# A two-layer-pair kernel on one core: the third chunk's second layers by Strassen's scheme, and its 1/rms applied behind the first layer

## The chip, the core and the metric

The kernel runs on one core of a Trainium2 chip. TensorE (PE) multiplies, VectorE (DVE), ScalarE (ACT) and GpSimd (POOL) work elementwise, SyncE (SP) issues the DMAs. The metric is the device time of one execution in microseconds; less is better.

## The reference

Attention with forget gates feeds two gated feed-forward networks; the second normalises its input by its root mean square.

```python
def _moe_ref(x, w_a, w_b, w_out):
    a = x @ w_a
    b = x @ w_b
    return (a * b @ w_out).astype(np.float32)
...
def _moe2_ref(x, w_gate, w_val, w_out, rms_g):
    rms = np.sqrt(np.mean(x * x, axis=-1, keepdims=True) + 1e-06)
    xn = x / rms * rms_g
    g = xn @ w_gate
    silu = g * (1.0 / (1.0 + np.exp(-g)))
    val = xn @ w_val
    return (silu * val @ w_out).astype(np.float32)
```

There are 2304 tokens, a model width of 512 and an inner width of 1536. Weights arrive as float64 and outputs are float32.

## The kernel before, in words

Tokens stand in columns. They are cut in three chunks of 576, 704 and 1024 (`CHUNKS`), and each chunk goes through both networks. `PHASES` gives the order of these passes: (network 0, chunk 0), (0, 1), (1, 0), (1, 1), (0, 2), (1, 2), numbered 0 to 5. The last two, phases 4 and 5, are the third chunk's.

Every float32 operand is split into a high part, rounded by ScalarE, and a low part, the remainder, on VectorE or GpSimd. A product is three matmuls (`triple`, L790 to L792): high by high, high by low, low by high.

The first layer of a chunk other than chunk 0 (`plan_wino`) uses Strassen's scheme in Winograd's form: for each f of 12 (128 inner rows each) seven blocks P1 to P7 of six matmuls stand for the two products with the two first weights, over two halves of columns (512 each in phases 4 and 5). `expand` makes the combinations of X that they read (sums L900, splits L907 and L910) in cells of E. PSUM bank m1 takes P1, P6, P5, P3 of one f in turn and is read between them; m2 takes P7 and P4, m3 P2. ScalarE takes a first value (L1027), VectorE adds the next (L1036), in phase 5 ScalarE's tanh (L1045) and L1049 make the gate, L1075 or L1036 the product, and L1126 and L1129 split it into G.

The second layer (`y_block`) is plain. It runs after each third of the f (`THIRDS`, four f each, `QF`): for four blocks i of 128 outputs and two column halves s, 12 matmuls (4 rows of G by three) into one bank; `out_part` puts the result into X (ACT for the first third, L824 or L826 for the others). In phase 3 the last third of the second layer is not done in place but held (`HELD`) and run at the end of phase 4, around the norm of phase 5. Its weights and those of the third chunk's y blocks come in two `wy` tiles.

The norm (`normed`) sums squares over partitions by matmuls (L1166), takes 1/sqrt by Newton steps on VectorE (L1162, L1178, L1181), spreads the result with diagonals (L1195) and multiplies X by it and by the gain (L1206). For phase 5 it stands between the second layer of phase 4 and the expansion of X.

Each engine runs its instructions in one fixed order. `Plan.order` lays it out ahead of the run: every operation has a cost, reads, writes and a due time (`prio`), and the earliest startable one goes next. An operation marked EITHER goes to VectorE or GpSimd.

Of the kernel before, what the change touches and what calls it, by code (L numbers as in the profile page):

```python
# [40 lines left out]

GRAIN = 32
# [6 lines left out]
    (((3, ALL, 0),), ((2, 0.1, 1.0, 0.7), (3, 0.1, 0.95, 0.3)), 20000),  # L49
# [16 lines left out]
HELD = 3  # L66
# [6 lines left out]
P_BUFS, PT_BUFS, RAW_BUFS, WY_BUFS = 4, 4, 2, 2  # L73
# [66 lines left out]
class Buf:  # L140
# [6 lines left out]
    def make(self):  # L147
        pool, shape, dtype = self.spec
        pool = pool() if callable(pool) else pool
        self.tile = pool.tile(shape, dtype, tag=self.tag, bufs=self.bufs, name=self.name)  # L150

# [166 lines left out]
class Kernel:  # L318
# [117 lines left out]

    def swap_3(self):
# [3 lines left out]
        self.G.append(pool.tile([128, 8 * WIDE], F32R, name="G2"))  # L441
# [35 lines left out]
    def cell_keys(self, b, t, c, m):  # L477
        return self.keys("E", *self.cell_at(b, t, c, m), slice(0, WIDTH[c]))

    @staticmethod  # L480
    def g_at(t, f, c):
        return int(c == 2), (t * QF + f % QF) * (WIDE if c == 2 else NARROW)

    def g(self, t, f, c, cols):
        x, o = self.g_at(t, f, c)
        return self.G[x][:, o + cols.start : o + cols.stop]

    def g_keys(self, t, f, c, cols):
        return self.keys("G", *self.g_at(t, f, c), cols)

# [5 lines left out]
    def blocks(self, p):  # L496
# [13 lines left out]
        out = [("P1", 0), ("P7", 0), ("P2", 0)]  # L510
        for f in range(FT):
            out += [("P6", f), ("P4", f)]
            nxt = [[(x, f + 1)] if f + 1 < FT else [] for x in ("P1", "P7", "P2")]
# [13 lines left out]
    def block_cost(self, p, x):  # L527
        c = PHASES[HELD if x[0] == "held" else p][1]
        if x[0] in ("y", "ab", "held"):
            return 12 * mm(size(c, x[-1]))  # L530
# [263 lines left out]
    def y_block(self, p, c, i, q, s, w, acc, t, e, first, last, m, after=()):  # L794
# [3 lines left out]
        for a, b in ((0, QF - 1), (QF - 1, QF)):  # L798

            def block(*_, a=a, b=b):  # L800
# [5 lines left out]
            made = self.op(  # L806
                PE, 3 * (b - a) * mm(n), block, reads=["late", (w, 0), (w, 1), *reads], writes=[acc],
                prio=t + 3000 + 0.75 * (e - t) * (a > 0), after=after,
            )
        self.out_part(p, m, c, i, s, first, last, acc, e)  # L810
        return made

    def out_part(self, p, m, c, i, s, first, last, acc, e):
# [6 lines left out]
        scale = 0.5 if m else 1.0  # L820

# [22 lines left out]
        ssq, keys_ = self.total(c, cols), self.total_keys(c, s)  # L844
        if i == 0:
# [3 lines left out]
            )  # L849
            return  # L850
# [5 lines left out]
        op(  # L856
            DVE, dve(n), lambda: nc.vector.tensor_tensor(out=ssq(), in0=ssq(), in1=q.tile[:, :n], op=ALU.add),
            reads=[q], writes=keys_, prio=e + 800, port=True,
        )
# [11 lines left out]
    def expand(self, p):  # L871
# [15 lines left out]
        x = lambda k, n: self.xc[c][:, 2 * k : 2 * k + 2, n * h : n * h + h]  # L887
        if m:
            has = lambda k, n: [y for i in (2 * k, 2 * k + 1) for y in pieces(c, n, "x1", c, i)]
        else:  # L890
            has = lambda k, n: [y for y, i, cols in self.x_parts[0, c] if i // 2 == k and cols.start < n * h + h and cols.stop > n * h]
        late = self.late2(p)
        of = lambda b, t: self.cell(b, t, c, m)
        used = self.used_x[m, c] = []
        cost = (dve(2 * h), pool2(2 * h))

        def add(d, out, a, b, how, reads, writes, start=True):
# [6 lines left out]
        def parts(b, src, reads, d):  # L904
# [7 lines left out]
            hi, lo = (self.cell_keys(b, t, c, m) for t in range(2))  # L912
            used.append(op(ACT, act(2 * h), high, reads=[*reads, *late], writes=hi, prio=t0 + d))
# [3 lines left out]
        h11, h12, h21, h22 = (has(k, n) for k in range(2) for n in range(2))  # L917
        at = lambda *k: ("at", c, m, *k)

        for k, n, y in ((0, 0, h11), (0, 1, h12), (1, 0, h21), (1, 1, h22)):  # L920
            self.plan.writer[at(k, n)] = op(None, 0, lambda: None, reads=y)
# [12 lines left out]


    def plan_wino(self, p, m, c):
# [4 lines left out]
        loaded, banks, a, turn, y_seen = {}, {}, {}, 0, []  # L941
        last_p = max(k for k, x in enumerate(blocks) if x[0] not in ("y", "held"))
# [25 lines left out]
        for k, x in enumerate(blocks):  # L968
# [4 lines left out]
            if x[0] in ("y", "held"):  # L973
                _, i, q, s = x
                m_, c_ = PHASES[HELD] if x[0] == "held" else (m, c)
                if s == 0:
                    all_ = x[0] == "y" and q == THIRDS - 1 and self.adjoins(p + 1)
                    w = loaded["y", m_, i, q] = self.w_tile() if p < SWAP_AT or all_ else self.tile(
                        [128, 2, 2, 256], "wy", WY_BUFS, F32R, pool=lambda: self.late_3
                    )  # L980
                    j = 2 * FT + 3 * i + q
                    op(
                        SP, 480, lambda z, m_=m_, j=j: nc.sync.dma_start(self.flat(z), self.wd[m_][j]),
                        reads=[("wd", m_, j), *([] if p < SWAP_AT else ["late3"])], writes=[(w, 0), (w, 1)], prio=t - 9000, nbytes=524288,
                    )
                w = loaded["y", m_, i, q]
                tags = ("m2", "m3") if q < THIRDS - 1 else ("m2", "m3", "m1", "m1")
                if p >= SWAP_AT:
                    acc = self.bank(*(("s", S_BANKS), ("tp", TP_BANKS))[turn % 2])
                else:  # L990
                    acc = self.m_bank(tags[turn % len(tags)])
                turn += 1
                after = [y_seen[KT - 1]] if x[0] == "held" else ()
                made = self.y_block(p, c_, i, q, s, w, acc, t, e, q == 0, q == THIRDS - 1, m_, after)
                if q == THIRDS - 1:
                    y_seen.append(made)
                if x[0] == "y" and q == THIRDS - 1 and i == KT - 1 and self.adjoins(p + 1):
                    self.normed(p + 1, c, s, e)
                    if s:
                        self.next_x(p + 1)  # L1000
                continue
            name, f = x
            kind, idx, b = use[name]
            w_ = load(kind, f, t)
# [18 lines left out]
            def grab(key):  # L1023
# [5 lines left out]
                op(ACT, act(h, 1), go, reads=[bank_, *self.late2(p)], writes=[y], prio=e)  # L1029

            def plus(key, mult=False, prio=0):
                y = a[f, key]

                def go(y=y, bank_=bank_):
                    z = y.tile[:, :h]
                    nc.vector.tensor_tensor(out=z, in0=bank_.tile[:, :h], in1=z, op=ALU.mult if mult else ALU.add)  # L1036

                op(DVE, dve(h), go, reads=[bank_], writes=[y], prio=e + prio)

            def gated(key):  # L1040
# [9 lines left out]

                op(ACT, act(h), tanh, reads=[y, *self.late2(p)], writes=[u], prio=e + 400)
# [695 lines left out]
```

## Time and the profile before

| | us |
|---|---|
| median of 3 runs | 1097.97 |
| lowest, highest | 1095.77, 1103.29 |
| the profiled execution | 1103.79 |
| its span in the profile | 1102.0 |

The span is the time from the first to the last recorded instruction of the profiled execution; 1.8 us of that execution lie around it. A matmul's row lasts until its modelled end, so rows of neighbours overlap.

### The profile page before, as it was taken

To read this page: it belongs to the slowest core of one execution; us is meant where nothing else is said; L and a number is where in the kernel's file an instruction comes from. 1 tells how busy PE (TensorE), PEld (TensorE's weight loads), DVE (VectorE), ACT (ScalarE), POOL (GpSimd) and SP (SyncE) were. 2 spreads that over 40 slices of the span, in tenths; PEclk is the share of its full clock that TensorE was granted. 3 is DMA by queue.
4 is the path that set the end of the run, shared out by engine and by line. 5 is a ranking of instruction groups with operands and counts; after the bars stand their busy time and mean duration, and the time that the engine had idled before them with its cause. 6 is when DMAs were issued, how large, how long until landed. Compare 5 with 4: busy or idle time off the path is not lost.

```text
span 1102.0 us, 19133 instructions
## 1 busy us (share of the span) xinstructions
PE 1070.9 (97%) x6794; PEld 951.8 (86%) x6794; DVE 726.3 (66%) x1684; ACT 549.6 (50%) x1215; POOL 212.9 (19%) x225
## 2 busy tenths in 40 slices
PE   9899999998999999989999999899999999999998
PEld 7577998997999999989899999788888888888886
DVE  6577578758758778889699685852343577516363
ACT  7677677755555468756665564522211224324040
POOL 3323244422303155433543010000000000000000
PEclk8999999999999999999999999999999999999999
DMA  7789878797767695677978773864544525535433
GB/s 219 218 303 298 304 244 289 244 333 250 259 217 262 227 350 199 216 252 250 309 256 312 247 267 140 306 210 135 170 153 156 169 90 204 180 131 184 120 119 115
DMA packets 93059, 245.41 MB, mean 223 GB/s; under 512 B 14460, under 2 KB 24908, under 8 KB 92964
## 3 DMA queue, kind: packets, MB, share of 16 engines
q1 hardware_dynamic: 92964, 244.19, 66.1%
q8 instruction: 54, 0.88, 0.3%
q14 instruction: 41, 0.34, 0.1%
HBM read 163.27 MB, written 80.88 MB: 222 GB/s over the span
## 4 chain that ended last, share of the span: by engine, by line
PE 74%; DVE 13%; DMA 6%; ACT 3%; issue 2%; SPq 1%; POOL 0%; DVEq 0%; ACTq 0%; POOLq 0%
PE m L790 17%; PE m L791 16%; PE m L792 16%; PE tp L1662 3%; PE s L1573 3%; PE tp L1268 3%; PE s L790 2%; PE tp L790 2%; PE tp L792 2%; PE s L792 2%; PE tp L791 2%; PE s L791 2%; DMA raw<-wb 1%; DVE G L1129 1%; DVE w L644 1%
## 5 line engine op out<-in xcount | busy, mean ns | idle before, releaser
L790 PE MATMUL m<-E,w 128*128 128x512 f32 (+3 forms) x672 | 235.8, 351 | 3.6 <-DVE a L1036 1.3
L792 PE MATMUL m<-E,w 128*128 128x512 f32 (+3 forms) x672 | 228.0, 339 | 0.0
L791 PE MATMUL m<-E,w 128*128 128x512 f32 (+3 forms) x624 | 213.8, 343 | 1.3 <-DVE E L910 1.3
L1036 DVE TENSOR_TENSOR a<-m,a 128x352 f32<-128x352 f32 (+1 forms) x192 | 115.2, 604 | 127.1 <-PE m L792 124.6
L790 PEld LDWEIGHTS m<-E,w 128*128 128x128 f32 x672 | 127.6, 190 | 19.9 <-issue 4.2
L1126 ACT ACTIVATE G<-a 128x352 fp32r<-128x352 f32 (+3 forms) x144 | 75.0, 521 | 135.4 <-DVE a L1036 75.0
L791 PE MATMUL m<-Eb,w 128*128 128x352 f32 (+3 forms) x432 | 141.2, 327 | 0.4 <-DVE Eb L910 0.4
L652 POOL TENSOR_TENSOR w<-w,w 128x512 fp32r<-128x512 f32 x72 | 98.0, 1366 | 220.7 <-ACT w L649 166.2
L792 PEld LDWEIGHTS m<-E,w 128*128 128x128 f32 x672 | 127.2, 189 | 10.3
L1027 ACT ACTIVATE a<-m 128x352 f32<-128x352 f32 (+1 forms) x144 | 74.9, 526 | 119.2 <-PE m L792 117.3
L790 PE MATMUL m<-Eb,w 128*128 128x352 f32 (+3 forms) x384 | 128.0, 333 | 5.3 <-DMA w<-wd 1.9
L791 PEld LDWEIGHTS m<-E,w 128*128 128x128 f32 x624 | 118.4, 190 | 13.1 <-DVE E L910 2.1
L792 PE MATMUL m<-Eb,w 128*128 128x352 f32 (+3 forms) x384 | 126.9, 330 | 0.0
L1129 DVE TENSOR_TENSOR G<-a,G 128x512 fp32r<-128x512 f32 (+3 forms) x132 | 81.1, 615 | 49.1 <-ACT G L1126 47.6
L790 PE MATMUL m<-G,w 128*128 128x352 f32 (+2 forms) x352 | 112.5, 320 | 0.5 <-DVE a L1036 0.5
L791 PE MATMUL m<-G,w 128*128 128x352 f32 (+2 forms) x352 | 108.6, 308 | 0.6 <-DVE G L1129 0.5
L792 PE MATMUL m<-G,w 128*128 128x352 f32 (+2 forms) x352 | 108.5, 308 | 0.2 <-POOL w L652 0.2
L1227 ACT ACTIVATE P<-P,mn 128x512 f32<-128x512 f32 (+4 forms) x128 | 76.2, 596 | 23.9 <-DVE mn L1220 21.9
L791 PEld LDWEIGHTS m<-Eb,w 128*128 128x128 f32 x432 | 81.4, 188 | 4.9 <-DVE Eb L910 0.7
L790 PEld LDWEIGHTS m<-Eb,w 128*128 128x128 f32 x384 | 72.3, 188 | 11.3 <-ACT a L1027 2.2
L792 PEld LDWEIGHTS m<-Eb,w 128*128 128x128 f32 x384 | 72.3, 188 | 4.2
L1220 DVE CUSTOM_DVE_ANT_0 P<-s,mask 128x512 f32<-128x512 f32 (+4 forms) x128 | 62.5, 495 | 12.1 <-PE s L1573 7.3
(180 smaller groups left out, 2080.4 us busy)
## 6 DMA issues: line engine op xcount, KB each, us to landing
w<-wd SPq DMA_DIRECT2D x88, 512.0 KB
wd<-w SPq DMA_DIRECT2D x72, 512.0 KB
ws<-w SPq DMA_DIRECT2D x48, 512.0 KB
w<-ws SPq DMA_DIRECT2D x48, 512.0 KB
wf<-w SPq DMA_DIRECT2D x48, 256.0 KB
raw<-wo SPq DMA_DIRECT2D x24, 512.0 KB
w<-wf SPq DMA_DIRECT2D x48, 256.0 KB
w<-wd SPq DMA_DIRECT2D x48, 256.0 KB
```

What stands on the lines that cost most here:

```text
L652: nc.gpsimd.tensor_tensor(out=w.tile[:, :, 1, :], in0=i32.tile.bitcast(F32), in1=w.tile[:, :, 0, :].bitcast(F32), op=ALU.subtract)
L790: mm_(o, wh, xh, start=start, stop=False)
L791: mm_(o, wh, xl, start=False, stop=False)
L792: mm_(o, wl, xh, start=False, stop=stop)
L1027: nc.scalar.activation(z[:, :h], bank_.tile[:, :h], AF.Copy)
L1036: nc.vector.tensor_tensor(out=z, in0=bank_.tile[:, :h], in1=z, op=ALU.mult if mult else ALU.add)
L1126: nc.scalar.activation(out(0), x(), AF.Copy)
L1129: self.engine(by).tensor_tensor(out=out(1), in0=x(), in1=out(0).bitcast(F32), op=ALU.subtract)
L1220: nc.vector.tensor_tensor_reduce(out=p.tile[:n, i * w : i * w + w], in0=s[i].tile[:n, :w], in1=masks[i][:n], scale=-0.125, scalar=mn.tile[ ...
L1227: nc.scalar.activation(o, o, AF.Exp, bias=mn.tile[:n, len(s) - 1 : len(s)], scale=-1.0, accum_out=sm.tile[:n, g : g + 1])
L1268: nc.tensor.transpose(ps.tile[:w, c : c + n], p.tile[:n, i * 128 : i * 128 + w], self.ident[:n, :n])
L1573: self.nc.tensor.matmul(x[:n, :e], q.tile[:, a:e], k.tile[:, :e], start=j == 0, stop=j == len(pairs) - 1)
```

## The change

It replaces, in two thirds (q = 0 and 1) of phases 4 and 5, the eight plain y blocks by a fast stage: for each of two pairs of output blocks, seven blocks ("z") of six matmuls after Strassen's scheme, in banks s (P1, P6, P5, P3) and tp (P2; P7, P4). Its operands are products G of four f, summed and split in three cells of Z that are written in turn (`fast_sums`, `fast_parts`), and sums of weights that are made in place (`fast_weights`). A fast stage stands one f after its third. The last third stays plain. In phase 5 the 1/rms no longer multiplies X. ScalarE multiplies X by the gain (`gained`), and each gate is scaled by 1/rms before the tanh and again after the gate, both for the gate and for the value's rows. `expand` works in half-size pieces there, and P1 and P2 of f = 0 and 1 come first. Phase 3's held third goes back to phase 3, with banks s and tp.

```diff
-HELD = 3
+FAST = (("P1", "one", 0), ("P2", "one", 1), ("P6", 1, 0), ("P7", 0, 0), ("P5", 0, 1), ("P4", "two", 1), ("P3", 1, 1))
+FAST_AFTER, CELL = 0, 2048
...
-        out = [("P1", 0), ("P7", 0), ("P2", 0)]
+        ahead = int(self.adjoins(p))
+        out = [*((x, f) for f in range(2) for x in ("P1", "P2")), ("P7", 0)] if ahead else [("P1", 0), ("P7", 0), ("P2", 0)]
...
-            if f % QF == QF - 1 and not (p == HELD and f == FT - 1):
+            if f == FT - 1 or (p < SWAP_AT and f % QF == QF - 1):
                 out += [("y", i, f // QF, s) for i in range(KT) for s in n]
+            elif p >= SWAP_AT and f and f % QF == FAST_AFTER:
+                out += [("z", i, f // QF - 1, k) for k in range(len(FAST)) for i in range(KT // 2)]
...
-        if p == HELD + 1:
-            out += [("held", i, THIRDS - 1, s) for i in range(KT) for s in range(len(CHUNKS[PHASES[HELD][1]][1]))]
...
+        def gained():
+            if self.late2(p):
+                op(
+                    ACT, act(n), lambda: nc.scalar.activation(x(), x(), AF.Copy, scale=self.gain[:, i : i + 1]), reads=["gain"],
+                    writes=keys, prio=e + 500,
+                )
...
+    def fast_sums(self, t):
+
+        k11, k12, k21, k22, kt2 = (self.gf_keys(n) for n in range(5))
+        for d, (out, ko), (a, ka), (b, kb) in (
+            (0, (0, k11), (1, k12), (0, k11)), (1, (1, k12), (3, k22), (1, k12)), (2, (4, kt2), (3, k22), (0, k11)),
+            (3, (2, k21), (2, k21), (4, kt2)),
+        ):
...
+    def fast_parts(self, n, src, t):
...
+        def high():
+            nc.scalar.activation(self.fast_cell(n, 0), self.gf(src), AF.Copy)
+
+        def low(by):
+            self.engine(by).tensor_tensor(
+                out=self.fast_cell(n, 1), in0=self.gf(src), in1=self.fast_cell(n, 0).bitcast(F32), op=ALU.subtract
+            )
...
+                    for k in range(2):
+                        self.triple(
+                            bank_.tile, w, idx, k, cells[0][:, k, :], cells[1][:, k, :], start and k == 0, k == 1,
+                            skip_group_check=True,
+                        )
...
+                def scaling(dt):
+                    if scaled:
+                        op(
+                            EITHER, (dve(h), pool2(h)), scale, reads=self.total_keys(c, int(key == 7)), writes=[y], prio=e + dt,
+                            port=True,
+                        )
+
+                scaling(200)
                 op(ACT, act(h), tanh, reads=[y, *self.late2(p)], writes=[u], prio=e + 400)
                 op(DVE, dve(h), go, reads=[u], writes=[y], prio=e + 800, port=True)
+                scaling(900)
...
-        for i in range(KT):
+        for i in () if late else range(KT):
```

The order of VectorE at three places follows. In names, xc2 is the third chunk's X, s and tp are banks, a2 a tile of a gate or value, u2 its tanh, nr the Newton steps' tile, ssq2 the sums of squares and later 1/rms, Z a fast cell, Y and xc1 hold products.

First, VectorE in phase 4's second third, second layer; before, one read for each of the eight y blocks:

```order
L826 TENSOR_TENSOR xc2_657<-s1944_10299,xc2_657 128x512
L826 TENSOR_TENSOR xc2_657<-tp1945_10321,xc2_657 128x512
L826 TENSOR_TENSOR xc2_657<-s1947_10335,xc2_657 128x512
L826 TENSOR_TENSOR xc2_657<-tp1948_10351,xc2_657 128x512
L826 TENSOR_TENSOR xc2_657<-s1950_10365,xc2_657 128x512
L826 TENSOR_TENSOR xc2_657<-tp1951_10381,xc2_657 128x512
L826 TENSOR_TENSOR xc2_657<-s1953_10395,xc2_657 128x512
L826 TENSOR_TENSOR xc2_657<-tp1954_10411,xc2_657 128x512
```

And now, in the fast stage that stands there:

```order
L884 TENSOR_TENSOR xc2_657<-s1959_10518,xc2_657 128x512
L884 TENSOR_TENSOR xc2_657<-s1960_10532,xc2_657 128x512
L1091 TENSOR_TENSOR Z_9640<-xc1_656,Z_9640 128x1024
L884 TENSOR_TENSOR xc2_657<-tp1961_10540,xc2_657 128x512
L1373 TENSOR_TENSOR G_655<-a21944_10419,G_655 128x512
L1373 TENSOR_TENSOR G_655<-a21947_10440,G_655 128x512
L1091 TENSOR_TENSOR Z_9640<-xc1_656,Z_9640 128x1024
L884 TENSOR_TENSOR xc2_657<-tp1962_10550,xc2_657 128x512
L884 TENSOR_TENSOR xc2_657<-s1959_10518,xc2_657 128x512
L884 TENSOR_TENSOR xc2_657<-s1960_10532,xc2_657 128x512
L1091 TENSOR_TENSOR Z_9640<-Y_9641,Z_9640 128x1024
L884 TENSOR_TENSOR xc2_657<-tp1963_10577,xc2_657 128x512
```

A bank is read two or three times now (s1959 above), with splits of fast cells (L1091) and of a later f's product (L1373) between the reads.

Second, VectorE at the norm of phase 5; before, from the Newton steps on the second half to X's scaling and the sums and splits of `expand`:

```order
L1162 TENSOR_SCALAR nr2011_10910<-s2010_10895 128x4
L1162 TENSOR_SCALAR nr2011_10910<-nr2011_10910 128x4 x3
L1178 TENSOR_TENSOR nr2011_10910<-nr2011_10910 128x4 x2
L1181 SCALAR_TENSOR_TENSOR nr2011_10910<-nr2011_10910 128x4
L1178 TENSOR_TENSOR nr2011_10910<-nr2011_10910 128x4 x2
L1181 SCALAR_TENSOR_TENSOR nr2011_10910<-nr2011_10910 128x4
L1178 TENSOR_TENSOR nr2011_10910<-nr2011_10910 128x4 x2
L1181 SCALAR_TENSOR_TENSOR nr2011_10910<-nr2011_10910 128x4
L1162 TENSOR_SCALAR xn22012_10931<-ident_105,nr2011_10910 128x128 x4
L1206 SCALAR_TENSOR_TENSOR xc2_657<-xc2_657,gain_85,s2013_10936 128x512 x3
L900 TENSOR_TENSOR xc2_657<-xc2_657 128x2x512
L824 SCALAR_TENSOR_TENSOR xc1_656<-s2015_10941,xc1_656 128x352
```

And now, from the last block of phase 4's second layer on:

```order
L884 TENSOR_TENSOR xc2_657<-tp2000_10951,xc2_657 128x512
L998 TENSOR_TENSOR E2_9212<-xc2_657,E2_9212 128x512
L988 TENSOR_TENSOR xc2_657<-xc2_657 128x512
L926 TENSOR_TENSOR ssq2_9211<-ssq2_9211,a22001_10986 128x512
L1243 TENSOR_TENSOR a22010_10996<-m32011_10988,a22010_10996 128x512
L1405 TENSOR_SCALAR nr2003_11018<-s2002_11001 128x4
L988 TENSOR_TENSOR xc2_657<-xc2_657 128x512
L998 TENSOR_TENSOR E_120<-xc2_657,E_120 128x512
L998 TENSOR_TENSOR E2_9212<-xc2_657,E2_9212 128x512
L998 TENSOR_TENSOR E_120<-xc2_657,E_120 128x512
L988 TENSOR_TENSOR xc2_657<-xc2_657 128x512
L1243 TENSOR_TENSOR a22014_11039<-m32015_11031,a22014_11039 128x512
```

The expansion's half-size sums (L988) and splits (L998) now stand ahead of the Newton steps, whose two halves run interleaved, and the scaling of X (L1206) is gone.

Third, VectorE in phase 5's first layer; before, from P4's add of one f on:

```order
L1036 TENSOR_TENSOR a22046_11137<-m22042_11092,a22046_11137 128x512
L1049 SCALAR_TENSOR_TENSOR a22046_11137<-u22048_11148,a22046_11137 128x512
L1075 TENSOR_TENSOR a22039_11080<-a22039_11080,a22046_11137 128x512
L1036 TENSOR_TENSOR a22043_11112<-m12038_10903,a22043_11112 128x512
L1129 TENSOR_TENSOR G2_9668<-a22039_11080,G2_9668 128x512
L1049 SCALAR_TENSOR_TENSOR a22043_11112<-u22052_11171,a22043_11112 128x512
L1036 TENSOR_TENSOR a22051_11156<-m32056_11174,a22051_11156 128x512
```

And now, from P4's add of f = 3:

```order
L1243 TENSOR_TENSOR a22052_11338<-m22048_11283,a22052_11338 128x512
L1260 TENSOR_TENSOR a22052_11338<-a22052_11338,ssq2_9211 128x512
L1243 TENSOR_TENSOR a22049_11301<-m12044_11261,a22049_11301 128x512
L1077 TENSOR_TENSOR xc1_656<-xc1_656 128x1024
L1256 SCALAR_TENSOR_TENSOR a22052_11338<-u22054_11363,a22052_11338 128x512
L1260 TENSOR_TENSOR a22049_11301<-a22049_11301,ssq2_9211 128x512
L1260 TENSOR_TENSOR a22052_11338<-a22052_11338,ssq2_9211 128x512
L1311 TENSOR_TENSOR Y_9641<-a22045_11276,a22052_11338 128x512
L1243 TENSOR_TENSOR a22057_11373<-m32062_11376,a22057_11373 128x512
L1256 SCALAR_TENSOR_TENSOR a22049_11301<-u22058_11387,a22049_11301 128x512
L1091 TENSOR_TENSOR Z_9640<-Y_9641,Z_9640 128x1024
L1260 TENSOR_TENSOR a22049_11301<-a22049_11301,ssq2_9211 128x512
```

Each gate and value is multiplied by ssq2 twice (L1260), and sums and splits of the fast stage (L1077, L1091) stand between.

## Rows read from the trace of the kernel before

**Rows 1.** The page: span, then busy time of each engine.
```profile
span 1102.0 us, 19133 instructions
PE 1070.9 (97%) x6794; PEld 951.8 (86%) x6794; DVE 726.3 (66%) x1684; ACT 549.6 (50%) x1215; POOL 212.9 (19%) x225
```

**Rows 2.** Windows: busy us and count of PE, PEld, DVE, ACT, POOL; PEclk; DMA; GB/s.
```profile
906.00:912.00 6.00, 4.20 (x23) 3.91 (x22) 5.52 (x8) 2.12 (x2) 0.00 (x0) 0.87 0.34 117
912.00:920.00 8.00, 8.00 (x43) 7.75 (x43) 8.00 (x9) 3.79 (x4) 0.00 (x0) 0.88 0.43 132
950.00:1000.00 50.00, 50.00 (x220) 40.93 (x219) 17.75 (x27) 17.60 (x29) 0.00 (x0) 1.00 0.46 149
1000.00:1050.00 50.00, 50.00 (x219) 40.94 (x218) 23.20 (x35) 12.80 (x21) 0.00 (x0) 1.00 0.48 152
```

**Rows 3.** Waits of PE, 640 us to the end: total, times, longest.
```profile
PE s L790 <- DVE xc L824: 1.8, 1, 1.8
PE m L790 <- ACT a L1027: 1.7, 1, 1.7
PE m L791 <- DVE E L910: 1.3, 2, 0.7
PE m L790 <- DMA w<-wd: 1.3, 1, 1.3
```

**Rows 4.** Timeline of PE at the norm: start, duration, what, [idle before, releaser].
```profile
901.54 0.95 PE L1166 MATMUL s<-ones,ssq 128*128 128x1 f32 x8
907.21 0.32 PE L790 MATMUL s<-G,wy 128*128 128x352 f32 x1
907.69 0.32 PE L790 MATMUL s<-G,wy 128*128 128x352 f32 x1
910.13 0.43 PE L790 MATMUL s<-G,wy 128*128 128x352 f32 x1 [1.80 <-DVE xc L824]
910.89 0.50 PE L790 MATMUL s<-G,wy 128*128 128x352 f32 x1
911.77 0.50 PE L790 MATMUL s<-G,wy 128*128 128x352 f32 x1
```

**Rows 5.** Timeline of DVE at the norm.
```profile
902.53 0.16 DVE L1162 TENSOR_SCALAR nr<-s 128x4 f32<-128x4 f32 x1
904.90 0.87 DVE L1162 TENSOR_SCALAR xn<-ident,nr 128x128 f32<-128x128 f32 x4
906.44 2.06 DVE L1206 SCALAR_TENSOR_TENSOR xc<-xc,gain,s 128x512 f32<-128x512 f32 x3 [0.67 <-PE s L1195]
```

**Rows 6.** Timeline: back-to-back passes of DVE and ACT, merged.
```profile
717.11 1.71 DVE L1036 TENSOR_TENSOR a<-m,a 128x512 f32<-128x512 f32 x3
...
897.90 1.16 ACT L853 ACTIVATE a<-xc 128x512 f32<-128x512 f32 x2 [1.76 <-DVE xc L826]
...
911.91 2.35 DVE L900 TENSOR_TENSOR xc<-xc 128x1024 f32<-128x1024 f32 x2
```

**Rows 7.** Timeline of DVE and POOL, 500 to 512 us.
```profile
502.79 0.41 DVE L1129 TENSOR_TENSOR G<-a,G 128x256 fp32r<-128x256 f32 x1
503.92 0.48 DVE L1112 TENSOR_TENSOR a<-m,a 128x320 f32<-128x320 f32 x1
...
509.49 3.18 POOL L652 TENSOR_TENSOR w<-w,w 128x512 fp32r<-128x512 f32 x2 [4.32 <-ACT w L649]
510.01 1.52 DVE L1129 TENSOR_TENSOR G<-a,G 128x256 fp32r<-128x256 f32 x1
511.45 0.48 DVE L1112 TENSOR_TENSOR a<-m,a 128x320 f32<-128x320 f32 x1
```

**Rows 8.** POOL on tile w: duration min/median/max in ns.
```profile
L652 POOL TENSOR_TENSOR w<-w,w x72: 1267/1294/2007, 16.4 to 571.4; 128x512 fp32r<-128x512 f32 x72
```

**Rows 9.** The chain: start, duration, what.
```profile
653.46 6.38 DMA w<-wd
```

More of the change, by code (lines that the diff above doesn't have):

```diff
@@ L435, in swap_2, with xc_free @@
         self.E.append(pool.tile([128, 5 * WIDE], F32R, name="E2"))
+    def xc_free(self):
+        return [x for s in range(2) for i in range(KT) for x in (*pieces(1, s, "x1", 1, i), *pieces(1, s, "ssq", False))]
     def swap_3(self):
@@ L792, in triple, with y_block @@
         mm_(o, wl, xh, start=False, stop=stop)
-    def y_block(self, p, c, i, q, s, w, acc, t, e, first, last, m, after=()):
+    def y_block(self, p, c, i, q, s, w, acc, t, e, first, last, m, has=None):
         cols, n = half(c, s), size(c, s)
@@ L820, in out_part @@
         scale = 0.5 if m else 1.0
+        urgent = 20000 if last and not m and self.late2(p) and (i, s) == (KT - 1, 1) else 0
+        e = e - urgent
         def more():
@@ L849, in out_part @@
             )
+            gained()
             return
@@ L855, in out_part, with total @@
         )
[L856 to L859, printed above, removed]
+        gained()
+        def total(by):
+            self.engine(by).tensor_tensor(out=ssq(), in0=ssq(), in1=q.tile[:, :n], op=ALU.add)
+        if self.late2(p):
+            op(EITHER, (dve(n), pool2(n)), total, reads=[q], writes=keys_, prio=e + 9000, port=True)
+        else:
+            op(DVE, dve(n), lambda: total(DVE), reads=[q], writes=keys_, prio=e + 800, port=True)
     def late2(self, p):
@@ L886, in expand, with has, combine, add @@
         h = size(c, 0)
[L887 to L891, printed above, removed]
         late = self.late2(p)
-        of = lambda b, t: self.cell(b, t, c, m)
         used = self.used_x[m, c] = []
-        cost = (dve(2 * h), pool2(2 * h))
-        def add(d, out, a, b, how, reads, writes, start=True):
+        x_at = self.x_at = getattr(self, "x_at", {})
+        parted = ((0, 1), (1, 2)) if self.adjoins(p) else ((0, 2),)
+        def has(k, n, a, e):
+            if m:
+                return [y for i in range(2 * k + a, 2 * k + e) for y in pieces(c, n, "x1", c, i)]
+            return [y for y, i, cols in self.x_parts[0, c] if i // 2 == k and cols.start < n * h + h and cols.stop > n * h]
+        at = lambda k, n, a: ("at", c, m, k, n, a)
+        for k in range(2):
+            for n in range(2):
+                for a, e in parted:
+                    self.plan.writer[at(k, n, a)] = op(None, 0, lambda: None, reads=has(k, n, a, e))
+        for a, e in parted:
+            x = lambda k, n, a=a, e=e: self.xc[c][:, 2 * k + a : 2 * k + e, n * h : n * h + h]
+            of = lambda b, t, a=a, e=e: self.cell(b, t, c, m)[:, a:e]
+            self.combine(x, of, lambda k, n, a=a: at(k, n, a), lambda b, t, a=a, e=e: self.cell_keys(b, t, c, m, a, e), (e - a) * h, t0 + 500 * a, late, used)
+    def combine(self, x, of, at, keys, size_, t0, late, used):
+        nc, op = self.nc, self.op
+        cost = (dve(size_), pool2(size_))
+        def add(d, out, a, b, how, reads, writes):
             def go(by):
@@ L940, in plan_wino @@
         norm = iter(self.plan_norm(p)) if p and PHASES[p - 1][0] == 0 and not self.adjoins(p) else iter(())
-        loaded, banks, a, turn, y_seen = {}, {}, {}, 0, []
-        last_p = max(k for k, x in enumerate(blocks) if x[0] not in ("y", "held"))
+        loaded, banks, a, turn, later = {}, {}, {}, 0, []
+        last_p = max(k for k, x in enumerate(blocks) if x[0][0] == "P")
+        scaled = self.adjoins(p)
+        if p == SWAP_AT:
+            op(None, 0, lambda: None, reads=[], writes=["late4", *self.xc_free()], prio=0)
+        if p >= SWAP_AT:
+            fast_at = {q: self.block_time(p, blocks.index(("z", 0, q, 0))) for q in range(THIRDS - 1)}
         def load(kind, f, t):
@@ L1083, in plan_wino, with times @@
             else:
-                plus(7, True, -500)
-                done(7, 1)
+                y = a.pop((f, 7))
+                def times(by, z, y=y, bank_=bank_):
+                    self.engine(by).tensor_tensor(out=z, in0=bank_.tile[:, :h], in1=y.tile[:, :h], op=ALU.mult)
+                soon(partial(done, 1, DVE, dve(h), times, y, [bank_]))
+                if p >= SWAP_AT and f % QF == QF - 1 and f < FT - 1:
+                    q = f // QF
+                    self.fast_sums(fast_at[q])
+                    for i in range(KT // 2):
+                        self.fast_weights(m, q, i, fast_at[q])
             if k == last_p and not self.adjoins(p + 1):
```

265 lines of the change are left out of this document (195 added, 70 removed).

## The prediction

> **What bounds the kernel now.** I read the page first: TensorE is busy 1070.9 of 1102.0 us and VectorE 726.3 [rows 1]. So time goes only where TensorE's work shrinks or where it stops waiting. Next I read the windows of the last 400 us, which the change touches. Between 950 and 1050 us TensorE never pauses and retires 220 and 219 matmuls of 512 columns in 50 us each: 0.228 us apiece [rows 2]. The row of one such matmul says 0.39, since they overlap; the spacing is the price. Then I asked what TensorE waits for from 640 us on: four causes, 6.1 us together [rows 3]. The 1.7 behind ScalarE's L1027 and the 1.3 behind a weight load lie ahead of the first changed instruction. The 1.3 behind L910 (third chunk's first expansion) and the 1.8 behind L824 (held blocks at the norm) lie inside the change. After that 1.8, three matmuls of 352 columns start 0.88 apart, against 0.48 before it [rows 4], and the granted clock of 906 to 920 us is 0.87 and 0.88 [rows 2], a mix of full and half speed: 0.13 x 6 + 0.12 x 8 = 1.7 us more.
>
> **What is removed.** The diff replaces 4 x 2 plain blocks of 12 matmuls by 7 x 2 blocks of 6, in two thirds of both layers: 96 - 84 = 12 fewer, four times, 48 in all. The program order agrees (TensorE 5849 rows, then 5801), so the work does go. 48 x 0.228 = 10.9 us. Phase 3's last third, now in place, puts 96 matmuls of 352 columns (0.16 each [rows 4], 15.4 us) between phase 3 and phase 4's first cell. The low parts that TensorE waited for are then ready: 1.3. The held blocks behind the norm are gone with their wait, 1.8, and the half-speed time, 1.7. Together 15.7 us.
>
> **What is added, off the path if VectorE keeps up.** Prices at the spacing of back-to-back rows: 512 columns on VectorE 0.57 to 0.60, 1024 columns 1.14, a 512-column ScalarE pass 0.58 [rows 6]. Each fast stage adds four sums and seven splits of 1024, eight 256-wide weight sums, four joins and four remainders. In phase 4 that is cheap: from its first block to the first fast stage the order gives VectorE 22.3 us in about 42. The third fast operand, T2, is the last needed: the last product, three sums, an add and a split are 5.8 us on VectorE, with a ScalarE pass of 1024 (twice 0.58) 7.0, while TensorE has 42 + 24 matmuls, 15 us. Cover 8 us; I count nothing, and if that cover were gone the excess would come 1:1.
>
> **The opening of phase 5** is where I expect the bill. After the last block of the second layer TensorE has ten P blocks of six before it must spread 1/rms: 60 x 0.228 = 13.7, and 0.95 for the sums [rows 4], 14.6 us. VectorE has, in this order, 16 passes of 512 (9.6), 26 small Newton steps of 0.18 (13 of them took 902.53 to 904.90 [rows 5]; 4.7) and eight diagonals at 0.21 [rows 5] (1.7): 16.0, plus 1.8 for its late start and waits on ScalarE and GpSimd (my allowance, 0.2 between engines): 17.8. TensorE is late by 3.2, less 0.9 of spreading done under the diagonals: 2.3. Then the first scaled product must free a bank of m1 for P1 of f = 2. VectorE has 15 more passes (8.7 us) against six blocks (8.2); with one wait for P4's bank and one for ScalarE to take P1 just ahead of P6, about 1.9. That makes 4.2. Before, the norm stood in front of X and cost the 1.8 already counted.
>
> **Scales and products.** Four scales for each f add 48 passes. From the spread to the end of f = 3 the order holds 46 passes of 512, three of 256 and three of 1024: 27.6 + 1.0 + 3.4 = 32.0 us of VectorE beside 168 matmuls, 38.3. It fits with 6 us to spare, unless GpSimd interferes. That engine has no work here now (0.00 in each window [rows 2]); the change gives it 24 operations from phase 4's end on, 19 of 512 columns at 1.29 [rows 8].
>
> A VectorE pass of 256 columns with both inputs in SBUF took 1.52 us beside a GpSimd subtraction, against 0.41 alone, while one that reads PSUM took its usual 0.48 [rows 7]. The Trainium skill, "SBUF — State Buffer", section "SBUF: two separate sides", says that a GpSimd operation and a VectorE one with two SBUF inputs lock a shared port pair for a whole instruction, and the loser blocks. By that rule up to 24 operations could each hold VectorE for 1.29 us, some 30 us of blocking as an estimate; the row agrees for the two-input pass.
>
> From rows 7 alone one block costs 1.1 us. Nothing in the trace shows so many two-input passes beside GpSimd, so bounds: 0 blocks, or one each time, 24 x 1.1 = 26 us of VectorE time, of which only what exceeds its slack reaches TensorE. I take two blocks in the opening (2.0 after rounding), 2.0 in f = 0 to 3 (its nine GpSimd operations, five of 1.29 and four of half that, are 9.1, so 41.1 against 38.3 if all block) and 2.5 for f = 4 to 8 and the four fast stages together.
>
> **Loads.** Each fast stage's four weight tiles are loaded in place when the last reader is done, and VectorE's first join waits in its queue behind that load, with bank reads queued behind the join. A load on the chain took 6.38 us [rows 9]. The first such tile comes free after P2's first block, 18 matmuls or 4.1 us into the stage, and the split behind its join is wanted by P4, 60 matmuls or 13.7 us in: 9.6 us for a load of 6.38, a join and a split of 1.7, so 1.5 to spare. I count nothing for it; a load slower by more would cost its excess. Small gaps now replace the 1.8 one; for the clock I keep 0.5 (between 0 and 1.7 [rows 2]).
>
> **Sum.** -10.9 - 1.3 - 1.8 - 1.7 + (4.2 + 2.0) + 2.0 + 2.5 + 0.5 = -4.5 us. The profiled execution took 1103.79 (1102.0 and 1.8 around it), so 1099.3 by it. It stood 5.8 above the median of 1097.97, so against that median I forecast 1093.5: no change that can be told, since a measurement of this kernel tells about 1%, 11 us.
>
> **Rivals.** *VectorE keeps up.* The opening costs 2, the rest 1 or less: -15.7 + 3 = -12.7, 1085. For it: only 17.75 of 50 us of VectorE are busy in 950 to 1000 [rows 2], and products have 9.6 us to be ready. Against it: the opening's 16.0 against 14.6 is counted from rows.
>
> *The gate chain sets phase 5's pace: slower than before.* Between P5's end and the P1 that needs its m1 bank again lie five blocks, 6.8 us. In them come add, scale, tanh, gate, scale, product: five passes of 0.69 (three take 2.06 [rows 5]), one of 0.6, six hand-overs at 0.2: 5.3. If half of VectorE's other 5 us for an f (2.5) and one block by GpSimd (1.1 [rows 7]) fall between, each f is 2.1 late, twelve times 25: -15.7 + 25 + 6.7 = +16, 1114. It decides from 1.7 us for each f: (11 + 15.7 - 6.7) / 12. Against it: in the order P1 often stands after P5, which gives the chain more than five blocks.
>
> *The fast stages stall.* P1, P6, P5 and P3 go on in the same bank, which is read between; TensorE returns after 12 matmuls, 2.7 us, and a read behind a 1.14 split and another read takes 0.2 + 1.14 + 0.6 + 0.69 + 0.2 = 2.8. With a join waiting for its load in front, 2 to 3 a stage, four times 2.7: the 10.9 are given back, the sum is -4.5 + 10.9 - 2.5 = +4, 1102.
>
> **How the numbers follow.** My forecast 0.50; VectorE keeps up 0.22; fast stages stall 0.14; gate chain 0.14. So faster by over 1% 0.22, within 1% 0.64, slower 0.14. The range takes the keep-up case with nothing lost beyond it (1082) and reaches past the stalling stages toward the gate chain, 1107, which leaves that chain's full price outside.
>
> **What would show it.** TensorE 48 matmuls fewer. No wait behind L998 near 715 us. Right, if after the second layer's last block TensorE waits 4 to 8 us in pieces (before P7 of f = 1 and P3 of f = 0, before the spread, before P1 and P6 of f = 2), and VectorE is over 0.8 busy in the 40 us behind. Wrong upward, if TensorE waits over 1.5 us in each f of phase 5 behind L1322 or L1243, or behind L884 and L882 in every fast stage. Wrong downward, if the waits from 710 us to the end sum to under 4 us.

## Result and profile after

The changed kernel ran in 1088.79 us (median of 11 runs, 1085.61 to 1092.39) beside 1099.66 for the kernel before on the same chip: ratio 0.9901, 95% interval 0.9875 to 0.9927, some 10.9 us less where 4.5 was forecast. The time lies in the range, and the sign is right; the losses charged against the gains were far too large (11.2 us, of which 2.6 came). The bound of 1% lies inside the interval, so the result stands between two of the prediction's classes.

The page of the changed kernel (span; busy time of engines), to set beside [rows 1]:

```profile
span 1087.5 us, 19283 instructions
...
PE 1058.2 (97%) x6746; PEld 939.5 (86%) x6746; DVE 814.6 (75%) x1805; ACT 573.5 (53%) x1244; POOL 256.1 (24%) x255
```

TensorE has 48 instructions fewer, as counted; VectorE has 88 us more work, GpSimd 43. What TensorE waits for from 702 us to the end (total, times, longest), beside [rows 3]:

```profile
PE m L846 <- DVE xc L1322: 1.3, 1, 1.3
PE m L846 <- ACT a L1234: 0.7, 1, 0.7
```

That is all: 2.0 us in 385, under the 4 us below which the prediction called itself wrong downward. Nothing is waited for behind L998 near 715, nor at the spread, nor in a fast stage. Windows of the opening of phase 5 and after (columns as in [rows 2]):

```profile
902.00:917.00 15.00, 15.00 (x81) 12.81 (x82) 14.21 (x50) 6.37 (x12) 3.00 (x2) 1.00 0.46 142
917.00:930.00 13.00, 10.98 (x47) 8.26 (x46) 13.00 (x21) 5.80 (x11) 4.95 (x4) 1.00 0.43 142
930.00:960.00 30.00, 30.00 (x131) 24.26 (x130) 29.56 (x40) 12.34 (x20) 10.11 (x6) 1.00 0.57 179
960.00:1000.00 40.00, 40.00 (x174) 32.41 (x173) 33.52 (x50) 18.16 (x29) 6.54 (x4) 1.00 0.47 150
1000.00:1050.00 50.00, 50.00 (x217) 40.46 (x216) 43.05 (x61) 17.38 (x26) 3.81 (x2) 1.00 0.48 153
```

The granted clock is 1.00 throughout, where it was 0.87 and 0.88 at the norm before. From 917 to 960 us VectorE is busy for 42.6 of 43 us and TensorE waits for it in one place only. The waits in the timeline of TensorE (start, duration, what, [idle before, releaser]):

```profile
924.50 0.40 PE L848 MATMUL m<-Eb,w 128*128 128x512 f32 x1
926.23 0.50 PE L846 MATMUL m<-E,w 128*128 128x512 f32 x1 [1.34 <-DVE xc L1322]
926.57 0.39 PE L847 MATMUL m<-E,w 128*128 128x512 f32 x1
...
928.59 0.49 PE L846 MATMUL m<-E,w 128*128 128x512 f32 x1 [0.69 <-ACT a L1234]
928.92 0.39 PE L847 MATMUL m<-E,w 128*128 128x512 f32 x1
```

After each wait the next start comes 0.33 to 0.34 later instead of 0.23, and then the pace is the usual one. With these restarts the opening costs about 2.6 us (worked out below).

Where the time went is read from starts of TensorE, whose instructions are the same in both kernels up to the first row of each pair below. Before, that row and the last one:

```profile
707.91 0.39 PE L790 MATMUL m<-E,w 128*128 128x512 f32 x1
...
1097.81 0.39 PE L792 MATMUL tp<-G,wy 128*128 128x512 f32 x1
```

After:

```profile
704.54 0.32 PE L846 MATMUL s<-G,w 128*128 128x352 f32 x1
...
1082.97 0.39 PE L848 MATMUL tp<-Z,G 128*128 128x512 f32 x1
```

From the one to the other it is 389.90 against 378.43: 11.5 less. By kind of work:

- the four stages that became fast ones: 4 x 21.81, now 4 x 19.54: -9.1
- the two last thirds, still plain: 22.25 and 21.59, now 22.29 and 22.05: +0.5
- phase 3's last third, 96 matmuls of 352 columns, held before and in place now: 19.1, now 15.3: -3.8
- the first layers' 1008 matmuls with their waits: 235.4, now 236.3: +0.9. An undisturbed stretch has 168 of them in 38.93 us, 0.2317 each. By that the expansion of phase 4 gives back 1.8 (186 matmuls took 44.9 us, not 43.1) and the opening of phase 5 costs 2.6 (168 took 41.6)

These sum to the -11.5. The other 3 us between the two spans lie ahead of this stretch, where the program is the same; the medians, 10.9 apart, don't show them.

One stage in the two timelines, its first matmul and the first behind it. Before (96 matmuls):

```profile
753.79 0.40 PE L790 MATMUL s<-G,wy 128*128 128x512 f32 x1
...
775.60 0.39 PE L790 MATMUL m<-E,w 128*128 128x512 f32 x1
```

After (84 matmuls):

```profile
773.62 0.40 PE L846 MATMUL s<-Z,G 128*128 128x512 f32 x1
...
793.16 0.39 PE L846 MATMUL m<-E,w 128*128 128x512 f32 x1
```

21.81 / 96 is 0.2272 us a matmul; 19.54 / 84 is 0.2326. Without any wait, each matmul left takes 5 ns longer.

### The profile page after: what moved, and what is told of

Its sections match the earlier page's. It is cut to its first block, busy times and chain, and to the rows that moved or that the text cites. A ratio compares the mean times of both kernels' runs of the same rounds, so it can differ in the third digit from the quotient of the medians.

```text
span 1087.5 us, 19283 instructions
## 1 busy us (share of the span) xinstructions
PE 1058.2 (97%) x6746; PEld 939.5 (86%) x6746; DVE 814.6 (75%) x1805; ACT 573.5 (53%) x1244; POOL 256.1 (24%) x255
## 4 chain that ended last, share of the span: by engine, by line
PE 76%; DVE 11%; DMA 7%; issue 2%; ACT 2%; SPq 1%; POOL 0%; DVEq 0%; ACTq 0%; POOLq 0%
PE m L846 17%; PE m L847 17%; PE m L848 17%; PE tp L1902 3%; PE tp L1508 3%; PE s L1813 3%; PE s L847 2%; PE s L848 2%; PE s L846 2%; PE tp L848 2%; PE tp L847 2%; PE tp L846 2%; DMA w<-wd 2%; DMA raw<-wv 1%; PE s L1839 1%
## 5 line engine op out<-in xcount | busy, mean ns | idle before, releaser
L847 PEld LDWEIGHTS m<-E,w 128*128 128x128 f32 x624 | 118.2, 189 | 11.2 <-issue 0.2
L1243 DVE TENSOR_TENSOR a<-m,a 128x352 f32<-128x352 f32 (+1 forms) x144 | 86.3, 602 | 50.6 <-PE m L848 50.1
L1370 ACT ACTIVATE G<-a 128x352 fp32r<-128x352 f32 (+3 forms) x100 | 47.1, 472 | 56.2 <-DVE a L1356 22.9
L846 PEld LDWEIGHTS m<-G,w 128*128 128x128 f32 x352 | 66.2, 188 | 2.8 <-issue 1.6
```

The lines of the kernel that those rows point to most:

```text
L846: mm_(o, wh, xh, start=start, stop=False)
L847: mm_(o, wh, xl, start=False, stop=False)
L1370: nc.scalar.activation(out(0), x(), AF.Copy)
```

## Experiments

Ratios are to the kernel before, on the same chip, with 95% intervals.

**Scheme and scaling apart.** Three kernels fill the table of scheme and scaling, all with phase 3's third in place. `no_fast` keeps the scaling of gates and has plain blocks in every third:

```diff
-            if f == FT - 1 or (p < SWAP_AT and f % QF == QF - 1):
+            if f % QF == QF - 1:
...
-            elif p >= SWAP_AT and f and f % QF == FAST_AFTER:
-                out += [("z", i, f // QF - 1, k) for k in range(len(FAST)) for i in range(KT // 2)]
```

(products go straight to their split, and the sums of products and of weights for the scheme are gone with it.)

> The changed kernel with all thirds of phases 4 and 5 done by plain blocks (96 matmuls a stage, not 84), the 1/rms still on gates and products, phase 3's third still in place. Theory (the matmuls' spacing goes with where their operands lie, so that the new cells cost 0.232 to 0.233 whatever the scheme): a stage takes 96 x 0.2325 = 22.3 us against 19.5 with the scheme, four stages +11, so about 1100, no better than the kernel before. Rival (plain blocks of twelve run at 0.227 as they did before, and blocks of six are what is slow): 21.8 a stage, +9, about 1098, and the rows of the plain stages show 0.227. In both the wait at the opening of phase 5 stays near 2 us.

`x_scaled` keeps the fast stages and puts the 1/rms back on X (with it go the separate gain, the half-size pieces and the new order of the first blocks):

```diff
-        scaled = self.adjoins(p)
+        scaled = False
...
-                    self.next_x(p + 1)
-                    for s in range(2):
-                        self.normed(p + 1, c, s, e + 4000)
+                    self.normed(p + 1, c, s, e)
+                    if s:
+                        self.next_x(p + 1)
...
-        for i in () if late else range(KT):
+        for i in range(KT):
```

> The changed kernel with the 1/rms put back on X before phase 5 (the fast stages and phase 3's third in place are kept). Theory (the scaling on gates is worth much more than the 1.8 us that the trace of before showed, because the held blocks that covered the chain to X are gone): from the last sums of squares to the first matmul on the expansion the kernel before took 16 us, 11 of them filled by held blocks; with nothing to fill it TensorE idles 12 to 15 us in one piece at the norm, then starts at half speed, and the 2 us behind products go: about +11 to +14, 1100 to 1103. Rival (as the prediction's ledger has it: only the 1.8 wait and 1.7 of half speed come back, and the opening's loss goes): +1, about 1090.

`held_in_place` is the kernel before with its third not held (and done in banks s and tp):

```diff
-HELD = 3
+HELD = -9
...
-                if p >= SWAP_AT:
+                if p >= SWAP_AT or (p == SWAP_AT - 1 and q == THIRDS - 1):
```

> The kernel before with one edit: phase 3's last third done in phase 3 instead of at the norm of phase 5. Theory: the 1.3 to 1.6 us behind the third chunk's expansion go, but the norm of phase 5 stands bare: some 12 to 15 us of TensorE in place of 11.2 filled with held work, of which 7.7 are paid for again in phase 3: net +6 to +9, so 1105 to 1109. Rival (the three gains of the prediction are independent of each other): -1.3 - 1.8 - 1.7, about 1095.

| third in place | 1/rms on X | 1/rms on gates |
|---|---|---|
| plain blocks | 1111.7, 1.0108 (1.0078 to 1.0137) | 1098.7, 1.0001 (0.9983 to 1.0019) |
| fast stages | 1103.2, 1.0033 (1.0012 to 1.0054) | 1088.8, 0.9901 (0.9875 to 0.9927) |

By these medians the scheme is worth 8.5 and 9.9 us, moving 1/rms 13.0 and 14.4, each uncertain by 3 to 4. The traces, from the start of phase 3's last third to the last matmul, give 399.6 and 387.7 for plain blocks and 393.1 and 378.4 for fast stages: 6.5 and 9.3 for the scheme, 11.9 and 14.7 for 1/rms. Part of the difference between the columns is that the plain stages don't stand in the same tiles: each takes 21.8 us in `held_in_place` and 22.3 in `no_fast`. With X scaled and the third in place, the fast stages alone would have made the kernel slower than it was. And `no_fast` stands at 1.0001: set against the kernel before and its held third, moving 1/rms gave nothing that can be told (2.2 us by the trace, with 1.9 paid for the new tiles). So the gain over the kernel before comes with the fast stages.

`x_scaled` came out at the upper end of its theory's 1100 to 1103, not at the rival's 1090. `held_in_place` came out about 12 over the kernel before (9.7 in its trace), more than the 6 to 9 expected, and far from the rival's 1095. The waits of `held_in_place` from 702 us on:

```profile
PE m L790 <- ACT E L907: 6.3, 1, 6.3
PE m L791 <- DVE E L910: 2.0, 2, 1.5
PE s L1195 <- DVE xn L1162: 1.9, 2, 1.3
```

10.2 us in place of the 1.8 that stood there. The two largest waits of `x_scaled`, at the same place:

```profile
PE m L846 <- ACT E L995: 7.2, 1, 7.2
PE m L847 <- DVE E L998: 2.2, 2, 1.5
```

And its windows behind (PEclk is the third number from the end):

```profile
912.00:920.00 8.00, 0.84 (x6) 0.58 (x4) 7.48 (x10) 3.66 (x4) 0.00 (x0) 0.56 0.10 41
920.00:930.00 10.00, 7.75 (x17) 5.22 (x17) 9.33 (x12) 4.72 (x7) 0.78 (x1) 0.50 0.00 0
```

After an idle stretch of 7.2 us the granted clock is 0.50, that is 1.2 GHz, and matmuls of 512 columns start 0.43 apart; after the 1.3 of the changed kernel it stayed at 1.00. So a long wait is paid for again behind its end. Holding the third or scaling gates are two covers for the same hole; taking one away needs the other. A kernel with both the held third and the fast stages wasn't tried: the held products stand in G, where the fast stages put weights.

The stage of `no_fast` that stands at the same place, 96 plain matmuls:

```profile
764.65 0.39 PE L844 MATMUL s<-G 128*128 128x512 f32 x1
...
786.93 0.39 PE L844 MATMUL m<-E,w 128*128 128x512 f32 x1
```

22.28 us, 0.2321 each: the theory's number, not the rival's 0.227. So it is not blocks of six that are slow; plain blocks of twelve are nearly as slow once their operands lie in the new tiles.

**Where operands lie.** Only offsets in a partition change in these.

`cells`, the low half of each Z cell 12 KB behind the high one:

```diff
...
-        return self.Z[:, n % 3 * CELL + t * WIDE : n % 3 * CELL + t * WIDE + WIDE]
+        return self.Z[:, (n % 3 + 3 * t) * WIDE : (n % 3 + 3 * t + 1) * WIDE]
```

> The changed kernel with the high and the low half of each cell of Z laid 12 KB apart in a partition instead of 4 KB (the same 24 KB, other offsets; nothing else moves). Before the change the plain blocks' halves lay 16 KB apart and ran at 0.227 us a matmul; the new cells, and the expansion's cells with 4 KB between the halves, run at 0.232 to 0.233. Theory (that distance sets the spacing): fast and plain stages of phases 4 and 5 fall to about 0.227, 528 x 0.0055 = 2.9 us less, 1086. Rival (it is the place of the weights, which now share tiles with the operands, or the address itself): the rows stay at 0.232 to 0.233 and the time at 1089.

1088.31, 0.9891 (0.9848 to 0.9934); the fast stages stay at 19.54 us. The theory, that the distance between the halves counts, falls.

`aligned` (by the program's allocation, G and the first layer's operands stood 32 bytes past a multiple of 128, Z 96):

```diff
-        self.gain = c.tile([128, KT], F32, name="gain")
+        self.gain = c.tile([128, 32], F32, name="gain")[:, 0:KT]
...
         self.Y = pool.tile([128, 3 * 1024], F32, name="Y")
+        pool.tile([128, 24], F32, name="pad")
```

> The changed kernel with all of TensorE's operands on multiples of 128 bytes in a partition (two paddings; they stand at 32 and 96 past one now). Theory (reads across a line's border cost the 5 ns): all 512-column matmuls of phases 4 and 5, 1008 of the first layers and 528 of the second, fall from 0.232 to 0.227 or below, some 7.7 us less, 1081. Rival (the offset within a line does not matter): spacing and time unchanged, 1089.

```profile
769.60 0.39 PE L847 MATMUL s<-Z,G 128*128 128x512 f32 x1
...
788.64 0.39 PE L847 MATMUL m<-E,w 128*128 128x512 f32 x1
```

19.04 us for 84 matmuls, 0.2267 each: every second-layer stage of phases 4 and 5 fell so (the plain last thirds to 0.2272), and the part of the stretch above that lies behind the third in place went from 362.2 to 359.2. Half of the theory failed: the first layers stayed at 0.2317. The time, 1087.84, ratio 0.9886 (0.9826 to 0.9946), can't tell 3 us by itself.

`aligned64` pads to 64 past a multiple of 128, `left_only` pads the left alone (Z stays at 96). Each has a profile and one time, so no interval.

> As the aligned kernel, but all operands 64 past a multiple of 128 bytes. Theory one (a line of 64 bytes counts): second-layer matmuls at 0.2267, as when aligned to 128. Theory two (128 counts): 0.232 to 0.233 as in the changed kernel. In both the first layers keep 0.2317.

> Only the weights' tile G, the first-layer operands and their weights on multiples of 128 bytes; the cells of Z, and those weights that lie in Z, stay at 96 past one. Theory one (the moving operand's place counts): all blocks of a fast stage stay at 0.231 to 0.234. Theory two (the weights' place counts): the eight of fourteen blocks with weights in G fall to 0.2267 and the six in Z stay at 0.2313. Theory three (the distance between the two counts): the Z blocks stay, those in G move to another value.

The times were 1086.97 and 1088.56; fast stages took 19.44 and 19.52 us, so neither helps as a whole. Single blocks of six take 1.36 us throughout in `aligned`, 1.36 to 1.40 in `aligned64`, 1.37 to 1.41 in `left_only`. There the nine blocks (not eight) with weights in G stay at 1.39 to 1.41, so the theory that the weights' place alone counts fails. So both operands on multiples of 128 gave 0.2267 in the fast stages, and less did not. It is not the whole rule: the plain stages of the kernel before ran at 0.2272 with both tiles 96 past one, as fast as the plain ones of `aligned`, and the first layers don't follow. What the rule is stays open.

The Trainium skill, "TensorE: Matmul & The Clock Gate", section "Step-by-step: what each phase is for", has the weights' load and the running matmul read SBUF through ports of their own, so that the one takes no read bandwidth from the other. That leaves open what an operand's offset costs. Here it costs something, 0.2326 against 0.2267 for the same instructions in the same order; no run here tells the two reads apart.

**GpSimd.** `no_gpsimd` keeps on VectorE every operation of phases 4 and 5 that the planner may choose:

```diff
-    def op(self, *a, **k):
-        return self.plan.op(*a, **k)
+    def op(self, eng, cost, fn, *a, **k):
+        if eng == EITHER and getattr(self, "now", 0) >= SWAP_AT:
+            eng, cost, fn = DVE, cost[0], partial(fn, DVE)
+        return self.plan.op(eng, cost, fn, *a, **k)
...
+        self.now = p
```

> The changed kernel with every operation of phases 4 and 5 that the planner could put on GpSimd kept on VectorE. Theory (GpSimd and VectorE block each other about one for one, so moving work off VectorE saved it next to nothing): VectorE's rows lose their stretched durations, its work grows by about as much, the waits at phase 5's opening stay 1 to 4 us, the time is within 2 us of the changed kernel's, 1087 to 1091. Rival one (the blocking is what makes the products late in the opening): the opening's wait goes to nothing, 1086. Rival two (without GpSimd VectorE is over-full in phase 5, as the sum of 41.1 against 38.3 us would have it the other way round): waits of 1 us in each of f = 0 to 3, 1092 or more.

1088.46, 0.9900 (0.9867 to 0.9933): the changed kernel's time, as the theory had it. Its page, to set beside the changed kernel's 814.6 us of VectorE and 256.1 of GpSimd:

```profile
PE 1059.0 (97%) x6746; PEld 939.5 (86%) x6746; DVE 818.9 (75%) x1835; ACT 574.6 (53%) x1244; POOL 213.9 (20%) x225
```

Thirty operations (21 of 512 columns, 9 of 256) are back on VectorE, which is busy 4.3 us longer for them; on GpSimd they took 42. At 0.60 us for 512 columns and 0.34 for 256, the spacing of back-to-back rows in this trace, they would be 15.7 us alone. More than half of what they take off is lost to operations that take longer beside GpSimd: in the changed kernel's trace VectorE's operations of phases 4 and 5 stand 8.4 us over their usual lengths, in this one none does. The scales L1260 on VectorE from 917 to 1060 us in the changed kernel (count | busy, mean ns | idle before), five more being on GpSimd:

```profile
L1260 DVE TENSOR_TENSOR a<-a,ssq 128x512 f32<-128x512 f32 x40 | 29.4, 749 | 0.3
```

The same scales without GpSimd (its line is 1263):

```profile
L1263 DVE TENSOR_TENSOR a<-a,ssq 128x512 f32<-128x512 f32 x44 | 29.4, 684 | 0.2
```

Forty beside GpSimd cost VectorE as much as forty-four without. The timeline of the changed kernel shows one such place:

```profile
920.46 1.68 POOL L1260 TENSOR_TENSOR a<-a,ssq 128x512 f32<-128x512 f32 x1
...
922.61 2.37 DVE L1260 TENSOR_TENSOR a<-a,ssq 128x512 f32<-128x512 f32 x2
...
923.36 1.07 POOL L1046 TENSOR_TENSOR ssq<-ssq 128x256 f32<-128x256 f32 x1
```

Two scales in 2.37 us; without GpSimd three took 1.88. TensorE's waits from 702 us on in `no_gpsimd`:

```profile
PE m L848 <- ACT a L1237: 0.7, 1, 0.7
```

The 1.3 behind L1322 is gone, and the first layer's stretch behind the spread takes 40.0 us, not 41.6. So the theory was wrong on the opening's waits, rival one is right on the place and too high on the gain, and rival two falls. But GpSimd isn't the only cause of the 1.3. `no_fast`, which keeps GpSimd on and has no weight sums, doesn't have it either; from 702 us on TensorE waits there for this alone:

```profile
PE m L844 <- ACT a L1230: 0.7, 1, 0.7
```

In the changed kernel VectorE makes three weight sums (L1031 twice, L1046) between the spread and L1322, 1.6 us by starts. Leaving out either these or GpSimd's work took the wait away, though each run also orders VectorE's work anew.

This is the rule that the prediction weighed: the Trainium skill, "SBUF — State Buffer", section "SBUF: two separate sides", has one of the two engines hold the shared ports for a whole instruction while the other blocks. The trace agrees that they hold each other up: a VectorE scale took 684 ns in the median and 1227 at most, and the same scale on GpSimd 1610 to 2212, where a GpSimd operation of that size took 1294 in the median before [rows 8]. Both pay.

**Order of the first blocks.** `no_ahead` has phase 5 start in the order of the other phases:

```diff
-        ahead = int(self.adjoins(p))
+        ahead = 0
```

> The changed kernel with the first layer of phase 5 in the order of the other phases (P1, P7, P2 of f = 0, and so on) instead of P1 and P2 of f = 0 and 1 first. Theory (ten blocks of six, 13.7 us, ahead of the spread of 1/rms are what covers VectorE's 16 us; without them the blocks wait for banks that VectorE must empty after the norm): TensorE waits 4 to 8 us more around the spread, 1093 to 1097. Rival (VectorE's chain is done in time either way, as the small waits measured there suggest): 1088 to 1090.

1091.78, 0.9921 (0.9891 to 0.9951), with the same two waits, 1.3 and 0.7, and the stretch behind the third 362.4 against 362.2. The rival holds: that order is worth nothing here that can be told.

**Both that shortened the trace.** `aligned_no_gpsimd` has the edits of `aligned` and `no_gpsimd`.

> The changed kernel with both edits that helped: operands on multiples of 128 bytes, and no work of phases 4 and 5 on GpSimd. Theory (the two gains are of different things and add up: second-layer matmuls at 0.2267 for 0.2325, 3.0 us, and the opening of phase 5 waiting 0.7 instead of 2.0 with its restarts, 1.5): 4 to 4.5 us below the changed kernel, 1084 to 1085. Rival (TensorE, faster by 5 ns a matmul, arrives earlier at the same products and waits for them; the median of the aligned one was only 1 below): 1087 or more, with new waits in phase 5.

1085.25, 0.9855 (0.9821 to 0.9889). The stretch behind the third is 357.8 us, 4.4 less than the changed kernel's: the theory's 4 to 4.5. Since the intervals touched, both kernels ran once more on one chip:

> The changed kernel itself, beside the next on the same chip, so that the two can be compared directly: 1089, ratio 0.990 to that before.

> The kernel with operands on multiples of 128 bytes and no work of phases 4 and 5 on GpSimd, once more. If the 4.4 us that its trace is shorter over phases 4 and 5 stand in the whole, its median lies 4 to 5 below the changed kernel of the same call, 1084 to 1085; if they are made up elsewhere, within 2 of it.

The changed kernel: 1089.45, 0.9921 (0.9906 to 0.9936). The other: 1082.30, 0.9864 (0.9842 to 0.9886), its page beginning

```profile
span 1077.6 us, 19257 instructions
...
PE 1052.4 (98%) x6746; PEld 935.5 (87%) x6746; DVE 818.7 (76%) x1835; ACT 574.2 (53%) x1244; POOL 212.5 (20%) x225
```

The intervals are apart now: this version beats both kernels. 4.4 us of it are shown in the trace (357.8 again, against 362.2 for the changed kernel each time); the medians lie 7.2 apart, and for the other 2 to 3 no cause is shown.

## Why the prediction was right, and where its terms were not

The forecast's sign and its range held, its size class (within 1%) only just, and so did the reason: less work and fewer waits on an engine that is busy 97% of the time, less a toll of VectorE and GpSimd at phase 5's opening. The gains of 15.7 came as 14.2 (9.1 + 1.8 + 3.8 - 0.5), the losses of 11.2 as 2.6. So the terms that failed are the losses, and the size of the toll is no success of the prediction: the range, 1082 to 1107, was wide enough for two of its three rivals as well, and by the prediction's own sign, waits of 4 to 8 us for right and under 4 for wrong downward, the 2.0 measured says wrong downward.

- **48 x 0.228 = 10.9.** The count was right, the result 9.1 less 0.5. The price was a mean over windows of first and second layers; the step assumed that what is left runs at the pace of what goes. The `aligned` run gives 84 x 0.2267 = 19.0, 2.8 a stage: 11.1, about the forecast's.
- **1.3 at the expansion, 1.8 and 1.7 at the norm.** Right in size: 1.8 with restarts, and 3.8. But they don't come by putting the third in place: `held_in_place` shows that this, without the scaling of gates, costs 12 us.
- **Spread late by 2.3.** Wrong: TensorE didn't wait. The step set 17.8 us of VectorE, and 2.0 more for GpSimd, against 14.6 of TensorE. The timeline of VectorE at this norm:

```profile
903.76 2.99 DVE L998 TENSOR_TENSOR E<-xc,E 128x512 fp32r<-128x512 f32 x3
...
909.87 0.58 DVE L1405 TENSOR_SCALAR nr<-nr 128x4 int32<-128x4 int32 x6
910.35 0.35 DVE L1421 TENSOR_TENSOR nr<-nr 128x4 f32<-128x4 f32 x3
910.70 0.69 DVE L1243 TENSOR_TENSOR a<-m,a 128x512 f32<-128x512 f32 x1
```

The six steps from 909.87 to 910.35 start 0.08 apart, where steps of one half took 0.18 each [rows 5]: the steps of two halves run interleaved, and one half's don't need the other's results. By starts, the 26 took 2.5 us, not 4.7. The 16 passes took 11.7, not 9.6: three GpSimd operations stand beside them, and the three splits from 903.76 took 2.99, where three passes alone take 1.88. Two of the three:

```profile
901.79 1.50 POOL L988 TENSOR_TENSOR xc<-xc 128x512 f32<-128x512 f32 x1 [1.39 <-ACT xc L907]
903.25 1.74 POOL L998 TENSOR_TENSOR E<-xc,E 128x512 fp32r<-128x512 f32 x1
```

So the 2.0 put down for GpSimd there was real on VectorE, and the Newton steps paid for it; the allowance of 1.8 was hardly used. VectorE needed 16.0 us and TensorE came after 15.7 (898.92 to 914.62), its sums having taken 1.7 rather than 0.95, since they are of both halves and the step counted one; the spread starts under the last diagonals.

- **P1 of f = 2 and P6, 1.9.** Right in place and size, 2.0 and restarts. But 1.3 of it went when GpSimd's work did, which the step had charged apart, and went too without the weight sums.
- **2.0 for f = 0 to 3, 2.5 for the rest, 0.5 of clock.** None of it came. VectorE was full from 917 to 960, as 41.1 against 38.3 had it; but a full VectorE is late for TensorE only where a bank or a product falls due, and none did behind 929 us. The two small waits didn't bring the clock down: it stayed at 1.00.
- **Loads counted at nothing, fast stages that don't stall.** Right: no wait stands behind L884, L882, L1091 or a weight load.

Of the rivals, "VectorE keeps up" (1085) described the mechanism best; its gain was too large by the price of the matmuls. The gate chain and the stalling stages showed nothing.

## What to carry to other kernels

When a change takes away work that covered a gap, price the bare gap, with the low clock behind it, and what covers it now: here, with the third in place, the algebra that shortens the dependency chain (12 to 15 us) was worth more than the arithmetic saved (6 to 10); against the cover that stood there before it gave next to nothing. Price removed matmuls by the stage that goes and what stays by its own stage: tile offsets alone moved a second-layer matmul of 512 columns between 0.227 and 0.233 us, which two paddings gave back. Giving thirty two-input operations to GpSimd, 42 us there, saved VectorE 4.3 us, since more than half of what it took off came back as longer operations beside it.

## What the runs showed of the hardware

- At full clock and without a wait, the time from start to start of matmuls of 512 columns depends on where tiles begin in a partition: 0.2326 in the changed kernel's fast stages, 0.2267 with the operands on multiples of 128 bytes, the same instructions in the same order.
- Small VectorE steps (128x4) of two independent chains, interleaved, start 0.07 to 0.12 us apart (2.5 us for 26), against 0.18 for one chain (2.37 us for 13).
- A GpSimd operation and a VectorE one, each with two SBUF inputs, slow each other: 44 scales on VectorE alone and 40 beside GpSimd took the same 29.4 us.
